# The first query block of an attention kernel: a split exponential, two projections placed earlier, a transpose on TensorE in place of DMA

## The chip, the core and the metric

The kernel runs on one core of a Trainium2 chip. The metric is the device time of one execution in microseconds (us); the time before is 1944.92 us, the median of three runs (1944.02 to 1945.15). Engines: PE (TensorE, matrix products into PSUM), ACT (ScalarE), DVE (VectorE), POOL (GpSimd) and SP (SyncE, here only an issuer of DMAs). They run their own instruction streams in order and wait for each other by semaphores.

## What is computed

x is 2048 rows of 640; there are 32 heads of width 192 with 2048 cached keys and values each.

```python
xn = layernorm(x)
q  = (xn @ wq), split into 32 heads of 192
p  = softmax(q @ k^T * 192**-0.5)
s  = (p @ v, heads joined) @ wo
h  = silu(xn @ w1) * (xn @ w3)
out = x + s * silu(h @ w2)
```

## The kernel before

**Tiles and stages.** The 2048 rows of x are four query blocks of 512, each of four row tiles of 128. Heads are worked one after the other; within a head the four query blocks; within a block eight *units* (p = 0 to 7), each of 256 keys. The list `stream` holds all 32 x 4 x 8 units, and n counts them; units 0 to 7 are head 0, block 0. After the heads come the rest of the gated FFN (L694 to L742) and the output product (L743 to L746).

**One unit.** `scores(n)` (L499, `emit_scores` L471) issues three pairs of products (L487, L488) into one PSUM tile of 1024 columns, then one exponential of the whole tile on ACT (L490), from PSUM into the bf16 tile pT2. Units 0 and 1 of the kernel begin with two full-height products (L483, L484) instead of two of the pairs. `values(n)` (L503) issues 16 products (L516) of pT2 with the values; the first eight read columns 0 to 511 of pT2 and the others columns 512 to 1023. The loop (L654) issues scores(n+2), then values(n), so the exponential runs while PE does other units. After unit 7 of a block DVE adds up the result (L525, L526) and scales it (L532, L533).

**PSUM turns.** The scores, every projection and the turned row tiles all take their PSUM tile from the pool `ps_st`, which has two buffers. A new tile there waits until the tile before the last has been read.

**x, normalized and turned.** For every row tile DVE computes statistics (`ln_stats`, L316, L317), POOL the reciprocal root (L327), DVE the normalized tile (`ln_norm`, L346). It then has to be transposed into `xnT`. In block 0 that is `ln_turn` (L349): ten PE products against an identity (L354) for two row tiles, then one copy from PSUM (L356). In the other blocks it is `ln_turn_dma` (L358): one transposing DMA for each row tile (L360), issued by SP. `swap_halves` (L362) then has SP copy both partition halves of a block crosswise into `xnS` (L364, L365).

**Projections.** `project0(qb)` (L403) makes the queries of head 0 for a block from xnT alone: ten full-height products (L410), a cast of one half on DVE (L429) and of the other on ACT (L430), and three DVE copies into `qC` (L413 to L415). `project(h, qb)` (L434) does it for a later head with 20 half-height products (L424) that read both xnT and xnS, the two casts, and three DMAs into qC that POOL issues (L377, L379). `project(1, 0)` is the one of head 1 for block 0; its result is first read by the scores of head 1.

**The order around the change.** It is written by hand (`tc.manual_schedule()`): each engine executes in the order in which the Python code issues.

- `head_start` (L571): loads, block 0 turned, project_first, scores(0), scores(1), statistics of block 1, its row tiles 0 and 1 normalized and their transposing DMAs issued. SP's queue in that order: the xnS copies of block 0, the second half of head 0's values, x of block 2, the two transposes, x of block 3.
- Unit 1 (`first_head`, L629): row tiles 2 and 3 of block 1 normalized, their two transposing DMAs, then swap_halves(1).
- Units 3 to 5: statistics of block 2 and the turning of its tiles 0 and 1; tiles 2 and 3 follow at unit 7.
- Unit 6: project0(1), then project(1, 0), then scores(8), the first scores of block 1, which read project0(1).
- Unit 8: project(1, 1), which reads xnT and xnS of block 1. Unit 12: project0(2).

**The check of the row sums.** After the last head DVE makes two columns of flags (L712 to L716); a product with a tile of ones (L717, L739) counts them, and the count decides at the end whether an exact second pass runs.

## Time and profile before

| what | value |
|---|---|
| time, median of 3 runs | 1944.92 us |
| the profiled execution's own time | 1944.92 us |
| its span in the profile | 1943.1 us |
| PE busy | 1928.0 us, 99% of the span |
| ACT, DVE, POOL busy | 1180.2, 653.6, 282.4 us |
| mean granted PE clock | 0.998 |

The span is what the hardware profiler saw from the first instruction to the last; 1.8 us of the time lie around it. "Busy" of an engine is the time in which it had at least one compute instruction in flight; matmuls overlap, so a busy PE is not a PE at its peak. In a timeline row the columns are start, duration, engine, line, operation, output<-inputs, shape and count; square brackets give the idle time of that engine just before the row and what ended it. In a row of DMA issues the last number is the time from issue to landing. The granted clock is the share of its full speed that TensorE was given.

### The profile page before, as it was taken

How to read it: one execution, taken by the hardware profiler on the slowest of the kernel's cores; microseconds unless marked ns; L12 is line 12 of the kernel's file. 1: busy time of each engine (PE TensorE's matmuls, PEld its weight loads, DVE VectorE, ACT ScalarE, POOL GpSimd, SP SyncE). 2: the span in 40 equal slices, each digit the busy share in tenths (PEclk: the TensorE clock that was granted, in tenths of full speed). 3: DMA queues.
4: the chain of work that ended last, by engine and by line, in shares of the span. 5: the costliest groups of instructions: out<-in, count | busy, mean ns of one | idle time of the engine just before them, and what ended most of it. 6: DMA issues, size and time to landing. Idle time of an engine off the chain costs nothing.

```text
span 1943.1 us, 59651 instructions
## 1 busy us (share of the span) xinstructions
PE 1928.0 (99%) x27263; PEld 1315.4 (68%) x27271; DVE 653.6 (34%) x996; ACT 1180.2 (61%) x1278; POOL 282.4 (15%) x501
## 2 busy tenths in 40 slices
PE   7999999999999999999999999999999999999998
PEld 5666666666666666666666666666666666577776
DVE  6433333333333333333333333333333334521111
ACT  5677676767676777676777777677767677210000
POOL 2111111111111111111111111111111110000000
PEclk9999999999999999999999999999999999999999
DMA  7743343323243434363434343434334220928882
GB/s 172 139 100 69 75 87 61 95 58 89 63 100 62 97 68 101 68 161 68 97 68 101 68 101 68 97 68 92 77 64 92 62 73 2 280 43 139 154 153 59
DMA packets 395987, 179.31 MB, mean 92 GB/s; under 512 B 342960, under 2 KB 384176, under 8 KB 395728
## 3 DMA queue, kind: packets, MB, share of 16 engines
q1 hardware_dynamic: 372480, 125.65, 31.2%
q0 software_dynamic: 19472, 45.71, 9.9%
q8 instruction: 215, 3.52, 0.8%
q10 hardware_dynamic: 3776, 4.06, 0.7%
q14 instruction: 44, 0.36, 0.1%
HBM read 52.82 MB, written 27.79 MB: 41 GB/s over the span
## 4 chain that ended last, share of the span: by engine, by line
PE 98%; DMA 1%; DVE 0%; ACT 0%; SPq 0%; issue 0%
PE obank L516 35%; PE st L487 33%; PE ps L424 14%; PE ps_s L111 11%; PE ps_f L728 3%; PE ps_gu L702 1%; DMA x_all<-in_A_x_dram 1%; PE st L488 1%; PE ps L410 0%; DMA xnT<-xn 0%; DVE stats L316 0%; ACT KW L277 0%; ACT xnT L356 0%; SPq L289 0%; PE pst L354 0%
## 5 line engine op out<-in xcount | busy, mean ns | idle before, releaser
L490 ACT ACTIVATE pT<-st 128x1024 bf16<-128x1024 f32 x1024 | 1046.2, 1022 | 249.8 <-PE st L488 234.2
L516 PEld LDWEIGHTS <-pT 64*128 64x128 bf16 x16384 | 711.4, 94 | 242.5 <-issue 0.4
L516 PE MATMUL obank<-vt,pT 64*128 64x193 bf16 x16384 | 849.5, 243 | 0.1
L487 PE MATMUL st<-qC,KW 64*128 64x512 bf16 x2046 | 605.6, 376 | 0.1
L525 DVE COPY osum<-obank 128x772 f32<-128x772 f32 x128 | 123.1, 962 | 789.0 <-PE obank L516 789.0
L488 PE MATMUL st<-qB,KW 64*128 64x512 bf16 x1024 | 385.0, 376 | 0.0
L487 PE MATMUL st<-qA,KW 64*128 64x512 bf16 x1022 | 384.3, 376 | 0.3 <-ACT pT L490 0.3
L488 PE MATMUL st<-qC,KW 64*128 64x512 bf16 x1022 | 384.3, 376 | 0.0
L488 PE MATMUL st<-qA,KW 64*128 64x512 bf16 x1022 | 384.3, 376 | 0.0
L487 PEld LDWEIGHTS <-KW 64*128 64x128 bf16 x3068 | 278.6, 94 | 153.2 <-issue 1.7
L424 PE MATMUL ps<-xnT,W 64*128 64x512 bf16 x1280 | 297.2, 376 | 0.0
L424 PE MATMUL ps<-xnS,W 64*128 64x512 bf16 x1280 | 296.4, 376 | 0.0
L488 PEld LDWEIGHTS <-KW 64*128 64x128 bf16 x3068 | 278.6, 94 | 0.6 <-issue 0.6
L377 POOL DMA_DIRECT2D qC<-qA x124 | 65.4, 527 | 1288.7 <-DVE rl_all L532 1269.0
L430 ACT CAST qB<-ps 128x512 bf16<-128x512 f32 x131 | 76.7, 585 | 235.0 <-PE ps L424 222.6
L111 PE MATMUL ps_s<-wo_sb,oT 128*128 128x384 bf16 (+3 forms) x1535 | 208.8, 299 | 0.1
L424 PEld LDWEIGHTS <-W 64*128 64x128 bf16 x2560 | 122.7, 94 | 122.2 <-issue 0.8
L111 PEld LDWEIGHTS <-oT 128*128 128x128 bf16 x1536 | 148.4, 98 | 60.4
L526 DVE TENSOR_TENSOR osum<-osum,obank 128x772 f32<-128x772 f32 x128 | 122.7, 959 | 13.4
L533 DVE TENSOR_TENSOR ostage<-osum,rl_all 128x768 bf16<-128x768 f32 x128 | 122.7, 958 | 4.5
L465 DVE SCALAR_TENSOR_TENSOR hT<-pt,qB 64x512 bf16<-64x512 bf16 x64 | 43.8, 684 | 198.3 <-ACT pt L464 198.3
L429 DVE CAST qA<-ps 128x512 bf16<-128x512 f32 x131 | 90.6, 692 | 30.2 <-PE ps L410 11.6
(84 smaller groups left out, 622.3 us busy)
## 6 DMA issues: line engine op xcount, KB each, us to landing
o_scr<-ostage SPq DMA_DIRECT2D x16, 1536.0 KB, 10.6
vt<-in_A_v_cache_dram SPq DMA_DIRECT2D x63, 384.0 KB, 6.0
qC<-qA POOLq DMA_DIRECT2D x248, 64.0 KB, 1.9
qC<-qB POOLq DMA_DIRECT2D x124, 64.0 KB, 2.4
wo_sb<-in_A_wo_dram POOLq DMA_DIRECT2D x1, 7680.0 KB, 30.7
W<-in_A_wq_dram POOLq DMA_DIRECT2D x32, 160.0 KB, 3.6
W<-in_B_w_dram POOLq DMA_DIRECT2D x32, 80.0 KB, 3.3
W<-in_A_wq_dram POOLq DMA_DIRECT2D x32, 80.0 KB, 3.0
```

The costliest lines, as they stand in the source:

```text
L111: nc.tensor.matmul(ps[:, 0:w], lhsT=oT[:, k, :], rhs=wo_sb[:, k, c0:c1], start=(k == 0), stop=(k == OC - 1))
L377: nc.gpsimd.dma_start(out=qC[0:64, half, :], in_=qAB[half][64:P, :])
L424: nc.tensor.matmul(ps[:, r * 512:(r + 1) * 512], lhsT=W[rows, j, :], rhs=xs[rows, j // 2, qs], start=(j == 0), stop=(j == 2 * DC - 1))
L429: a = nc.vector.tensor_copy(out=qAB[0][:], in_=ps[:, 0:512])
L430: b = nc.scalar.copy(out=qAB[1][:], in_=ps[:, 512:1024])
L487: nc.tensor.matmul(st2[:, 0:512], lhsT=ka, rhs=qa, start=r == 0 and nr == 3, stop=r == nr - 1)
L488: nc.tensor.matmul(st2[:, 512:1024], lhsT=kb, rhs=qb2, start=r == 0 and nr == 3, stop=r == nr - 1)
L490: nc.scalar.activation(out=pT2[:], in_=st2[:], func=ACT.Exp, scale=att_scale)
L516: nc.tensor.matmul(obanks[r][:, j * 256:j * 256 + DH + 1], lhsT=pT2[r * 64:(r + 1) * 64, t * 512 + j * P:t * 512 + (j + 1) * P], rhs=vt[r ...
L525: nc.vector.tensor_copy(out=osum[:], in_=ov[0])
L526: nc.vector.tensor_tensor(out=osum[:], in0=osum[:], in1=ov[1], op=ALU.add)
L533: nc.vector.tensor_tensor(out=ostage[:, qb * 4:qb * 4 + 4, hg * DH:(hg + 1) * DH], in0=osum[:, :, 0:DH], in1=rl.unsqueeze(2).to_broadcast( ...
```

## The change

Five edits:

1. The very first exponential (head 0, block 0, unit 0) is issued as two, of 512 columns each; all others stay whole.
2. In the first turn of the loop (n = 0) values(0) is issued ahead of scores(2); in all other turns scores come first, as before.
3. Row tiles 2 and 3 of block 1 are turned by PE and a DVE copy (`ln_turn(1, 1, ...)`), after values(3), in place of the two transposing DMAs after values(1). swap_halves(1) moves with it, from unit 1 to unit 3.
4. project(1, 0) moves from unit 6 to unit 3 (ahead of scores(5)), and project0(1) from unit 6 to unit 5 (ahead of scores(7)).
5. The tile of ones is 128 x 128 instead of 128 x 2, and the count is a product 128 x 2 instead of 2 x 2; row 0 is read as before.

```diff
         pT2 = pp.tile([P, 1024], BF16, tag="pT2", name="pT2")
-        nc.scalar.activation(out=pT2[:], in_=st2[:], func=ACT.Exp, scale=att_scale)
+        parts = 2 if (h, qb, p) == (0, 0, 0) else 1
+        w = 1024 // parts
+        for c in range(parts):
+            nc.scalar.activation(out=pT2[:, c * w:(c + 1) * w], in_=st2[:, c * w:(c + 1) * w], func=ACT.Exp, scale=att_scale)
...
         if qb == 0 and p == 1:
-            for i in (2, 3):
-                ln_norm(1, i, nc.vector)
-                ln_turn_dma(1, i)
-            swap_halves(1)
+            ln_norm(1, 2, nc.vector)
+            ln_norm(1, 3, nc.vector)
         if qb == 0 and p == 3:
             ln_stats(2, 0)
+            ln_turn(1, 1, nc.vector.tensor_copy)
+            swap_halves(1)
...
-        if h == 0 and qb + 1 < NQB and p == (6 if qb == 0 else 4):
+        if h == 0 and qb == 0 and p == 3:
+            project(1, 0)
+        if h == 0 and qb + 1 < NQB and p == (5 if qb == 0 else 4):
             project0(qb + 1)
-        if h == 0 and qb == 0 and p == 6:
-            project(1, 0)
-        scores(n + 2)
-        values(n)
+        for step in (values, scores) if n == 0 else (scores, values):
+            step(n + 2 if step is scores else n)
...
-    ones = fsb.tile([P, 2], BF16, tag="ones", name="ones")
+    ones = fsb.tile([P, P], BF16, tag="ones", name="ones")
...
-            nc.tensor.matmul(cnt[0:2, 0:2], lhsT=ones[:], rhs=okb[:], start=True, stop=True)
+            nc.tensor.matmul(cnt[:, 0:2], lhsT=ones[:], rhs=okb[:], start=True, stop=True)
```

On PE the order from unit 3 on becomes: project(1, 0), scores(5), values(3), the ten turning products, scores(6), values(4), project0(1), scores(7), values(5), scores(8), values(6), scores(9), values(7), project(1, 1). On DVE the cast of project(1, 0) and the copy of the turned tiles come ahead of most of block 2's statistics, with one row tile's statistics between them. On SP the two xnS copies of block 1 come straight after the load of x's block 3, ahead of all transposes of block 2. On POOL the three qC DMAs of project(1, 0) come ahead of block 2's reciprocal roots.

## The prediction

> **What bounds the kernel now.** First the page's busy line and chain of waits: PE is busy for 99% of the span and 98% of the chain. So time can only be won where PE is idle, slowed, or does less.

> ```profile
> PE 1928.0 (99%) x27263; PEld 1315.4 (68%) x27271; DVE 653.6 (34%) x996; ACT 1180.2 (61%) x1278; POOL 282.4 (15%) x501
> ...
> PE 98%; DMA 1%; DVE 0%; ACT 0%; SPq 0%; issue 0%
> ```

> Second, the table of waits: PE's only long one is a single wait at L410, in project0(1). Third, the timeline there, then PE's clock in short stretches (columns: stretch, length, busy us of the five engines, granted clock, DMA share, GB/s).

> ```profile
> 22.59 0.85 PE L516 MATMUL obank<-vt,pT 64*128 64x193 bf16 x16
> ...
> 28.69 0.58 PE L410 MATMUL ps<-xnT,W 128*128 128x512 bf16 x1 [5.25 <-DMA xnT<-xn]
> 29.50 3.59 PE L410 MATMUL ps<-xnT,W 128*128 128x512 bf16 x8 [0.22 <-issue]
> ...
> 45.46 2.33 PE L410 MATMUL ps<-xnT,W 128*128 128x512 bf16 x9
> ```
> ```profile
> 24.40:25.40 1.00, 0.00 (x0) 0.00 (x0) 0.93 (x4) 0.01 (x1) 0.05 (x1) 1.00 0.07 12
> 25.40:26.40 1.00, 0.00 (x0) 0.00 (x0) 0.97 (x4) 0.00 (x0) 0.64 (x1) 0.85 1.01 410
> 26.40:27.40 1.00, 0.00 (x0) 0.00 (x0) 1.00 (x3) 0.00 (x0) 0.00 (x0) 0.50 1.17 297
> ...
> 30.40:31.40 1.00, 1.00 (x4) 0.39 (x3) 0.00 (x0) 0.00 (x0) 0.00 (x0) 0.50 0.96 202
> ...
> 33.00:33.50 0.50, 0.50 (x7) 0.25 (x8) 0.37 (x1) 0.38 (x1) 0.00 (x0) 1.00 1.22 202
> ```

> PE stops at 23.44, 5.25 us long, for the last of block 1's transposing DMAs. And it pays twice: its clock halves at about 26.1 (a stretch with mean 0.85 is 0.7 at 1.0 and 0.3 at 0.5) and is back only near 32.9, so project0(1) takes 4.4 us (28.69 to 33.08) against 2.2 for the same product at 45.46. The hole is worth 5.25 + 2.2 = 7.45 us. Fourth, SP's transfers, by their issue and landing:

> ```profile
> 11.55 0.61 SPq L365 DMA_DIRECT2D xnS<-xnT  x1
> xnS<-xnT SPq DMA_DIRECT2D x1, 320.0 KB, 8.5
> ```
> ```profile
> 19.40 1.21 SPq L360 DMA_TRANSPOSE xnT<-xn  x1
> xnT<-xn SPq DMA_TRANSPOSE x1, 6.3
> ```

> Block 0's second xnS copy lands at 11.55 + 8.5 = 20.05. Block 1's transposes land at 23.5, 25.7 (19.40 + 6.3), 27.7 and 28.55. These landings are the limits of the new order.

> **Price list.** Scores of a unit 0.65 us (three pairs, 0.21 each in the chain, 0.216 with its gaps); values 0.67; project and project0 2.16; exponential 1.02; turning products 0.72 for ten (second L354 group), their copy 0.82 (L356 on DVE). A unit is 1.32 on PE, more than the exponential, so ACT follows PE.

> **Edits 1 and 2 (split exponential, values(0) first).** ACT starts at 14.07. Halves of 128x512 are not in the trace; the nearest rows are the casts of that size, 0.585, so the two end at 15.24 if nothing overlaps, against 15.09 whole. PE can begin values(0) when scores(1) is issued, 14.8, do eight products until 15.15, wait for the second half, and end at 15.6; scores(2) to 16.25; scores(3) waits for exponential 1, 16.25; from there 1.32 per unit. Unit 3 begins at 18.88 instead of 19.08: 0.2 won. Bounds: 0.15 us lost (ACT's extra work lands on the path whole) to 0.35 won (the 0.28 idle before scores(2) and the gaps after it). But what follows is a wait with a fixed end, so edits 1 and 2 are worth nothing in the sum; only were that wait gone would 0.2 show.

> **Edit 4, first half (project(1, 0) at unit 3).** In the profile it never waited, at 33. Now PE reaches it at 18.88 and its second product reads xnS of block 0, landed at 20.05; PE restarts about 0.1 later (28.55 to 28.69 in the chain), 20.15. A new wait of 1.27 us. Its weights landed at 17.0 (9.60 + 7.4). All that feeds this copy is issued before 12.2, ahead of every edit, so I keep its landing. Queued behind the waiting product: everything on PE, thus exponential 5.

> **Edit 3 and the rest, on PE from 20.15.** project(1, 0) to 22.31; scores(5) 22.96; values(3) 23.63; turning, new, 0.72, to 24.35 (its buffer is free when the casts of project(1, 0) end, 23.1); scores(6) 25.00 (exponential 5, after the cast on ACT, ends at 24.2); values(4) 25.67. It no longer meets the landing of the second half of the values at 21.2, which in the profile held values(4) for 0.36 us.

> Then project0(1), which needs two things. The DVE copy of the turned tiles: DVE casts 22.4 to 23.1, has one tile's statistics ahead (1.05; its x landed at 22.84), is free at 24.25, copies 24.5 to 25.35. And the second transposing DMA, landed at 25.7: PE starts at 25.80, a wait of 0.13, ends at 27.96. I take 25.7 although two transposes behind it are gone; bounds 25.0 (it moves no more once these are gone, and the DMA engines were nearly idle from 24.4 to 25.4) to 27.0 (the POOL copies of project(1, 0), 64 KB each and 1.9 to 3.0 from issue to landing, now share the DMA engines from 23.1 on; half of 2.7 if they hold it up).

> scores(7) and values(5) to 29.28. scores(8) needs the casts and the three qC copies. In the profile, project(1, 0) lay between and hid them; that cover of 2.16 is now 1.32. DVE reaches the cast only at 28.45 (statistics and two normalizations of block 2 are ahead), the third copy ends 1.54 later (33.13 to 34.67 in the profile), 29.99, so the last pair ends at 30.27 instead of 29.93: 0.34 lost; bounds 0.1 (DVE on time) to 1.1 (one more statistics group late). values(6), scores(9), values(7): 32.26.

> There project(1, 1) starts; in the profile at 37.82. **Won: 37.82 - 32.26 = 5.56 us.** In other words: the hole's 7.45, plus 0.36 and 0.2, less the new waits 1.27, 0.13 and 0.34 and the turning 0.72.

> **What is late next.** project(1, 1) reads xnS of block 1: SP issues its copies when both the second DMA and the DVE copy are in, 25.8 and 26.4; with the 3.6 and 4.5 us that they took in the profile they land by 30.9, 1.4 ahead. Behind them in SP's queue are block 2's transposes, 2 us earlier than before for the first two; the last two follow unit 7's DVE work (L525, L526, L346) at the same distance as before. They must land before project0(2). In the profile the last was issued at 41.73, took 3.5, landed at 45.2, and PE came at 45.46: 0.2 us spare, which I expect to hold, being five units of the same order later. POOL's qC copies of project(1, 0) are first read at head 1. From unit 8 on all engines' orders are unchanged.

> **Edit 5.** The count is one product: the ACT rows of L733 around it are 3.47 apart (1693.41 to 1696.88) instead of 3.26, so it costs 0.21 on PE. Its weight load goes from 2 to 128 columns: 0.08 to 0.098 by the rows; bounds 0.2 won to 0.1 lost; I take 0. The larger memset (0.06 for 2 columns, 0.20 for 128 x 128 on POOL) lies in DVE's 0.36 us of idle time before L734; without that cover 0.14.

> [...] PE's clock survived the idle 1.02 us before the first turning products (clock 1.00 from 5 to 10) and fell 2.7 us into the long hole. So waits of 1.27 and 0.13, five us apart, should leave it up. [...]

> **Rivals.**
> - *The clock falls all the same*, since waits of 1.27, 0.13 and 0.34 and the turning crowd into 11 us. Price: the 2.2 us that ten halved products lost; 1941.6. Against it: the clock held from 5 to 18 with PE busy 83 to 93%.
> - *The landings slip.* Every us that the xnS copy or the second transpose lands later costs 1 us: both are on the path, nothing covers them. At 1.7 us the change is within 0.2%; about 1941.5 to 1943.
> - *Slower: the hole moves to block 2.* Its transposes had 0.2 us to spare and now stand behind xnS copies that wait for a DVE copy. If the last lands 8.5 us after issue (as that xnS copy did) instead of 3.5, PE stands 4.8, the clock falls (2.2 more): +7.0 - 5.56 = +1.4, 1946.3. It decides from 3.6 us of lateness on (3.4 of standing and 2.2). Against: at 34 us of the new order the queue is as empty as at 40 of the old one.

> **How the numbers follow.** Against the profiled execution's own 1944.92 (span 1943.1 and 1.8 around it), also the median: 1944.92 - 5.56 = 1939.4. Its own range, by the bounds, 1938.4 to 1940.9. Chances: main case 0.83, clock 0.07, landings 0.07, block 2 0.03. The range reaches to the clock's case: 1938.3 to 1941.7. 0.2% is 3.9 us, about what a measurement tells from no change; below 1941.0 lie the main case and a little of the others: faster 0.85, same 0.12, slower 0.03.

> **What would show it.** No wait of PE over 1.5 us behind unit 0; one of about 1.3 us at L424 ended by the xnS copy, near 20.1; project0(1) of 2.2 us at clock 1.00, starting near 25.8; project(1, 1) near 32.3. Wrong if a clock of 0.5 appears, or if a wait over 2 us stands before project0(2).

## The result and the profile after

The changed kernel takes 1938.31 us, the median of six runs (1937.68 to 1938.64), against 1944.88 for the kernel before beside it (1943.27 to 1945.15): a ratio of 0.9968, 95% interval 0.9955 to 0.998. That is 6.6 us won; 1939.4 was forecast, with a range of 1938.3 to 1941.7. The profiled execution took 1938.20 us; its span is 1936.4, 6.7 less than before.

The busy line of the page after:

```profile
PE 1926.6 (99%) x27273; PEld 1315.6 (68%) x27281; DVE 654.6 (34%) x997; ACT 1180.0 (61%) x1279; POOL 282.5 (15%) x501
```

PE's busy time fell by only 1.4 us (1928.0 before), though the span fell by 6.7: the rest was idle time. The timeline after, with SP's second xnS copy of block 0, its second transposing DMA of block 1, the two projections, the turning and, last, project(1, 1); then the landings of that copy and of that DMA:

```profile
11.57 0.61 SPq L365 DMA_DIRECT2D xnS<-xnT  x1
...
18.84 0.38 PE L424 MATMUL ps<-xnT,W 64*128 64x512 bf16 x1
19.05 0.39 PE L424 MATMUL ps<-xnS,W 64*128 64x512 bf16 x2
...
19.42 1.20 SPq L360 DMA_TRANSPOSE xnT<-xn  x1
...
22.61 0.73 PE L354 MATMUL pst<-ident_bf,xn 128*128 128x128 bf16 x10
...
24.84 2.32 PE L410 MATMUL ps<-xnT,W 128*128 128x512 bf16 x9
...
31.04 0.38 PE L424 MATMUL ps<-xnT,W 64*128 64x512 bf16 x1
```
```profile
xnS<-xnT SPq DMA_DIRECT2D x1, 320.0 KB, 7.4
...
xnT<-xn SPq DMA_TRANSPOSE x1, 5.3
```

No row has the brackets of a long wait any more. project0(1) starts at 24.84 instead of 28.69 and takes 2.3 us instead of 4.4. PE's clock in the stretches that held the hole (columns as in the prediction):

```profile
24.00:26.00 2.00, 1.87 (x23) 1.13 (x21) 1.93 (x7) 1.02 (x1) 0.44 (x2) 1.00 0.95 360
26.00:28.00 2.00, 2.00 (x20) 0.87 (x19) 1.89 (x6) 0.58 (x1) 0.31 (x1) 1.00 1.08 213
```

The granted clock stays at 1.00. Two landings differ from the forecast. The xnS copy landed at 11.57 + 7.4 = 18.97, not at 20.05, so project(1, 0) went on at 19.05 after 0.2 us instead of 1.27. The second transposing DMA landed at 19.42 + 5.3 = 24.7, not at 25.7, so project0(1) could start at 24.84, though PE came to it 1.1 us earlier than forecast. project(1, 1) starts at 31.04, 6.78 earlier than in the profile before (37.82).

### The profile page after: what moved, and what is told of

It is laid out like the page before. It is cut to its first block, busy times and chain, and to the rows that moved or that the text cites. A ratio compares the mean times of both kernels' runs of the same rounds, so it can differ in the third digit from the quotient of the medians.

```text
span 1936.4 us, 59669 instructions
## 1 busy us (share of the span) xinstructions
PE 1926.6 (99%) x27273; PEld 1315.6 (68%) x27281; DVE 654.6 (34%) x997; ACT 1180.0 (61%) x1279; POOL 282.5 (15%) x501
## 4 chain that ended last, share of the span: by engine, by line
PE 99%; DVE 1%; DMA 0%; ACT 0%; issue 0%; DVEq 0%; ACTq 0%
PE obank L519 35%; PE st L487 34%; PE ps L424 14%; PE ps_s L111 11%; PE ps_f L731 3%; PE ps_gu L705 1%; PE st L488 1%; PE ps L410 0%; DVE stats L316 0%; DMA x_all<-in_A_x_dram 0%; PE ps L391 0%; PE pst L354 0%; PE pk L271 0%; DVE xn L346 0%; ACT pT L493 0%
## 5 line engine op out<-in xcount | busy, mean ns | idle before, releaser
L493 ACT ACTIVATE pT<-st 128x1024 bf16<-128x1024 f32 (+1 forms) x1025 | 1046.1, 1021 | 250.2 <-PE st L488 234.0
L424 PE MATMUL ps<-xnT,W 64*128 64x512 bf16 x1280 | 297.2, 376 | 0.0
L424 PE MATMUL ps<-xnS,W 64*128 64x512 bf16 x1280 | 296.0, 376 | 0.0
L424 PEld LDWEIGHTS <-W 64*128 64x128 bf16 x2560 | 122.9, 94 | 121.4 <-issue 0.2
```

What stands on the lines that cost most here:

```text
L424: nc.tensor.matmul(ps[:, r * 512:(r + 1) * 512], lhsT=W[rows, j, :], rhs=xs[rows, j // 2, qs], start=(j == 0), stop=(j == 2 * DC - 1))
L493: nc.scalar.activation(out=pT2[:, c * w:(c + 1) * w], in_=st2[:, c * w:(c + 1) * w], func=ACT.Exp, scale=att_scale)
```

## The experiments

**Edit 3 alone.** Which part carries the gain?

```diff
         if qb == 0 and p == 1:
-            for i in (2, 3):
-                ln_norm(1, i, nc.vector)
-                ln_turn_dma(1, i)
-            swap_halves(1)
+            ln_norm(1, 2, nc.vector)
+            ln_norm(1, 3, nc.vector)
         if qb == 0 and p == 3:
             ln_stats(2, 0)
+            ln_turn(1, 1, nc.vector.tensor_copy)
+            swap_halves(1)
```

> Edit 3 alone: row tiles 2 and 3 of block 1 turned by PE at unit 3, both projections still at unit 6, first exponential whole, count as before. Theory (the hole is one wait for two transposing DMAs plus the halved clock that follows it, and edit 3 removes both): PE reaches project0(1) near 24.2 and waits 0.5 to 1.6 us for the second of the two DMAs that remain, clock 1.00 throughout, project0(1) 2.2 us; 4.6 to 6.2 us faster than before, 1938.7 to 1940.3. Rival (the gain is the earlier place of project(1, 0), which fills the hole): at most 2.5 us faster.

1939.69 us against 1944.33, ratio 0.9977 (0.9968 to 0.9987): 4.6 us, at the lower edge of what the theory gave and far over the rival's 2.5. Its timeline:

```profile
21.03 0.81 PE L354 MATMUL pst<-ident_bf,xn 128*128 128x128 bf16 x10 [0.27 <-DVE xn L346]
...
23.96 0.37 PE L487 MATMUL st<-qA,KW 64*128 64x512 bf16 x1 [0.70 <-DVE xnT L356]
25.39 2.33 PE L410 MATMUL ps<-xnT,W 128*128 128x512 bf16 x9
```

Without project(1, 0) at unit 3, the turning comes before DVE has the row tile (0.27 idle), and the scores after it wait for DVE's copy out of the shared PSUM pool (0.70). The wait of 0.5 to 1.6 us that was expected at project0(1) itself did not come: the second transposing DMA landed at 23.4, before PE was there. project0(1) again takes 2.3, and the clock stays at 1.00. So taking two row tiles off the DMA path is most of the gain. The remaining 1.4 us to the changed kernel is the other edits together; that the move of project(1, 0) fills just these two waits is how the rows read, and was not measured by itself.

**The hole kept, PE kept running in it.** Is the slow product after the hole the clock's doing? The added products are extra work, overwritten at once.

```diff
         ps = ps_st.tile([P, 1024], F32, tag="st2", name="ps0")
+        for i in range(24 if qb == 1 else 0):
+            nc.tensor.matmul(ps[:, 0:512], lhsT=W[:, 0, :], rhs=xnT[:, 0, 0:512], start=True, stop=True)
```

> The kernel before, with 24 products of 512 columns (5.2 us) issued ahead of project0(1) into the same PSUM tile and then overwritten: extra work in the hole, nothing else. Theory (the 4.4 us of project0(1) after the hole are the halved clock, price 2.2 us): the wait for the last transposing DMA stays, the clock stays at 1.00, project0(1) takes 2.2; 1.2 to 2.2 us faster than before, 1942.7 to 1943.7, although PE does more. Rival (project0(1) is slow for another reason, such as reading xnT just written): no faster than before, or slower.

1942.65 us against 1944.33, ratio 0.9992 (0.9983 to 1.0001). The time alone just fails to exclude no change; the rows do not leave it open:

```profile
23.58 5.35 PE L409 MATMUL ps<-xnT,W 128*128 128x512 bf16 x23
28.77 2.32 PE L412 MATMUL ps<-xnT,W 128*128 128x512 bf16 x10
```
```profile
26.00:27.00 1.00, 1.00 (x6) 0.46 (x5) 1.00 (x3) 0.00 (x0) 0.00 (x0) 1.00 1.28 287
27.00:28.00 1.00, 1.00 (x6) 0.48 (x5) 0.93 (x4) 0.00 (x0) 0.00 (x0) 1.00 0.12 27
```

project0(1) (L412 here) starts as late as ever, at 28.77, and takes 2.32 instead of 4.4, at a clock of 1.00. Its price, about 2 us of the hole's 7.45, is shown. The time shows less of it (1.7), since in this trace the last transposing DMA landed at 27.84 and the added products held PE for some 0.8 us more. So xnT was not quite as freshly written here as before; but in the changed kernel's trace project0(1) starts 0.14 us after its DMA's landing, just as before (28.55 to 28.69), and takes 2.32 too. That rules the rival out.

**Edit 4 alone.** Does filling the hole from the front help, if the DMA path stays?

```diff
-        if h == 0 and qb + 1 < NQB and p == (6 if qb == 0 else 4):
+        if h == 0 and qb == 0 and p == 3:
+            project(1, 0)
+        if h == 0 and qb + 1 < NQB and p == (5 if qb == 0 else 4):
             project0(qb + 1)
-        if h == 0 and qb == 0 and p == 6:
-            project(1, 0)
```

> Edit 4 alone: project(1, 0) at unit 3 and project0(1) at unit 5, all four row tiles of block 1 still by transposing DMA. Theory (the end of the hole is the landing of the fourth transpose, 27.5 to 28.6, whatever lies before it, and a wait of over 2.7 us halves the clock): a wait of 3.2 to 4.7 us, project0(1) at half clock; 0.3 to 1.6 us faster than before. Rival (the clock stays up, since the hole is shorter): 2.6 to 3.7 us faster.

1944.8 us against 1944.33, ratio 1.0003 (0.9994 to 1.0012): nothing won, though 0.3 to 1.6 was expected.

```profile
29.26 0.59 PE L410 MATMUL ps<-xnT,W 128*128 128x512 bf16 x1 [4.79 <-DMA xnT<-xn]
30.06 3.62 PE L410 MATMUL ps<-xnT,W 128*128 128x512 bf16 x8 [0.22 <-issue]
```

The wait is 4.79, since the last transposing DMA landed only at 29.12 in this trace; with all four DMAs it landed between 27.69 and 28.68 in the others. The clock is at half from PE's return at 29.26 until 34.2, 5.0 us, longer than in any other trace here. The rival, a clock that stays up, is out. Edit 4 depends on edit 3: 4 without 3 is worth nothing, 3 without 4 and the others leaves 1.4 us.

**Edits 1 and 2 alone, and taken away.**

```diff
-        nc.scalar.activation(out=pT2[:], in_=st2[:], func=ACT.Exp, scale=att_scale)
+        parts = 2 if (h, qb, p) == (0, 0, 0) else 1
...
-        scores(n + 2)
-        values(n)
+        for step in (values, scores) if n == 0 else (scores, values):
+            step(n + 2 if step is scores else n)
```

> Edits 1 and 2 alone: first exponential in two halves, values(0) ahead of scores(2). Theory (PE gets to unit 3 about 0.2 us earlier, and the hole, whose end is a landing, takes all of it): no difference, within 0.3 us of before; the hole starts 0.2 us earlier and ends at the same landing. Rival (the two exponentials cost ACT 0.15 us on the path, or the gain carries through): a shift of the whole span by 0.15 to 0.4 us, one way or the other.

On the kernel before: 1943.82 us against 1944.33, ratio 0.9998 (0.9989 to 1.0007), no difference. The hole swallows it:

```profile
28.01 0.38 PE L410 MATMUL ps<-xnT,W 128*128 128x512 bf16 x1 [4.79 <-DMA xnT<-xn]
28.56 3.45 PE L410 MATMUL ps<-xnT,W 128*128 128x512 bf16 x8 [0.17 <-issue]
```

Taken back out of the changed kernel (the same diff reversed):

> The changed kernel with edits 1 and 2 undone: first exponential whole, scores(2) ahead of values(0). Theory (what edits 1 and 2 win in front is kept, since no wait with a fixed end is left behind them but the 0.1 us for the second transposing DMA): PE idle 0.28 us before scores(2) again, project(1, 0) starts 0.2 us later, the whole 0.1 to 0.3 us longer than the changed kernel, 1938.4 to 1938.6: not to be told apart by time, only by PE's rows between 14 and 26 us. Rival (the two edits carry a good part of the gain): 0.6 us or more longer.

1938.47 us; the changed kernel in the same series, 1938.27. The 0.28 us of idle time is back:

```profile
15.45 0.37 PE L487 MATMUL st<-qA,KW 64*128 64x512 bf16 x1 [0.28 <-ACT pT L490]
...
19.38 0.38 PE L424 MATMUL ps<-xnT,W 64*128 64x512 bf16 x1
...
25.09 2.32 PE L410 MATMUL ps<-xnT,W 128*128 128x512 bf16 x10
```

Counted from the first scores' product (13.39 here, 13.10 in the changed kernel), project(1, 0) starts after 5.99 instead of 5.74: 0.25 us. But project0(1) starts after 11.70 here and 11.74 in the changed kernel: there the two landings had taken the 0.25 back. So in these two traces edits 1 and 2 win nothing that lasts, against the theory that their gain is kept. In time the two kernels cannot be told apart, as expected.

**Edit 5 alone.**

```diff
-    ones = fsb.tile([P, 2], BF16, tag="ones", name="ones")
+    ones = fsb.tile([P, P], BF16, tag="ones", name="ones")
...
-            nc.tensor.matmul(cnt[0:2, 0:2], lhsT=ones[:], rhs=okb[:], start=True, stop=True)
+            nc.tensor.matmul(cnt[:, 0:2], lhsT=ones[:], rhs=okb[:], start=True, stop=True)
```

> Edit 5 alone on the kernel before: tile of ones 128 x 128, count product 128 x 2. Theory, as read from the changed kernel's trace (the ACT rows of the FFN around the count stand 3.28 us apart there, 3.47 before): the same 3.28 here, so 0.2 us less on PE; the time 0 to 0.4 us shorter, within the spread of the kernel before. Rival (the wider weight load costs its 0.02 us and nothing is won): 3.47 or 3.49.

1943.94 us against 1943.97, ratio 1.0 (0.9991 to 1.0009). In the trace of this run, the ACT rows ahead of, at and after the count:

```profile
1688.89 0.49 ACT L733 ACTIVATE ft<-ps_f 128x384 bf16<-128x384 f32 x1 [1.76 <-PE ps_f L728]
...
1691.78 0.10 PEld L739 LDWEIGHTS <-ones 128*128 128x128 bf16 x1
...
1692.15 0.49 ACT L733 ACTIVATE ft<-ps_f 128x384 bf16<-128x384 f32 x1 [1.76 <-PE cnt L739]
...
1695.43 0.49 ACT L733 ACTIVATE ft<-ps_f 128x384 bf16<-128x384 f32 x1 [1.79 <-PE ps_f L728]
```

They are 3.26 and 3.28 apart; before, 3.26 and 3.47. So 0.19 us is won although 64 times as many weight columns are loaded (0.10 instead of 0.08 us). What went is a pause ahead of the load; the row in the trace before was

```profile
1693.24 0.08 PEld L739 LDWEIGHTS <-ones 128*2 128x2 bf16 x1 [0.26 <-issue]
```

Why the narrow load had this pause of 0.26 us and the wide one none was not tried.

**The changed kernel once more.**

> The changed kernel once more, unchanged, for its spread and for a second look at the landings. Theory (the xnS copy's 20.05 in the one profiled execution of the kernel before was about 1 us later than usual, and the wait of 1.27 us that the prediction built on it does not come): xnS lands near 19.0, no wait over 0.3 us at project(1, 0), time 1937.7 to 1938.8. Rival (the landing differs from execution to execution by 1 us or more): a wait of up to 1.3 us at project(1, 0) in this profile, and a spread of the times of more than 1.5 us.

1938.27 us, median of seven (1938.07 to 1939.32), against 1943.97: ratio 0.997 (0.9959 to 0.9981). The profiled one of the seven is the slowest, 1939.32, and it is the one that settles the matter:

```profile
11.82 0.61 SPq L365 DMA_DIRECT2D xnS<-xnT  x1
...
19.10 0.38 PE L424 MATMUL ps<-xnT,W 64*128 64x512 bf16 x1
20.47 0.39 PE L424 MATMUL ps<-xnS,W 64*128 64x512 bf16 x2 [0.99 <-DMA xnS<-xnT]
...
26.11 2.33 PE L410 MATMUL ps<-xnT,W 128*128 128x512 bf16 x10
...
32.33 0.38 PE L424 MATMUL ps<-xnT,W 64*128 64x512 bf16 x1
```
```profile
xnS<-xnT SPq DMA_DIRECT2D x1, 320.0 KB, 8.6
```

Here the copy lands at 20.42, PE stands between 19.10 and 20.47 as forecast (0.99 of it not covered by the product in flight), and project(1, 1) starts at 32.33; the forecast said 32.26, and 1939.4 for the whole. So the rival of this run holds in its main point: the landing differs from execution to execution (the times spread by 1.25 us, less than the 1.5 that it named). The traces of all kernels that issue this copy in this place give two groups: 20.05 and 20.42 (the kernel before, this run), and 18.9 to 19.5 in the eight others. PE came to project0(1) after the second transposing DMA here (24.47), without a long wait.

**A later xnS copy.** Is it true that nothing covers project(1, 0) in its new place? The first attempt exchanged the wrong pair:

```diff
+        load_v(0, (1,))
         swap_halves(0)
...
-        load_v(0, (1,))
         load_x(2)
```

> The changed kernel with one pair of SP's issues exchanged: the second half of head 0's values (384 KB) ahead of the two xnS copies of block 0. Theory (in its new place project(1, 0) has no cover: every us that the xnS copy lands later than about 19 is one us on the path): the copies land 1.3 to 2.1 us later, near 20.3 to 21.1; PE waits 1.3 to 2.1 us at project(1, 0), of which the 0.1 us wait before project0(1) gives back its part; 1.1 to 2.1 us longer than the changed kernel, 1939.4 to 1940.4; the clock stays at 1.00. Rival (the queue is shared anyway, the landing does not move, or the wait before project0(1) takes its place): within 0.4 us of the changed kernel.

1941.47 us (1939.42 to 1944.43), ratio 0.9989 (0.998 to 0.9998). It does not answer the question: SP no longer holds this load behind the wait for block 0's turning, so it is issued before 10 us (at 12.22 in the changed kernel's trace), and the first scores begin 1.5 us later, at 14.82. That the load competes with the first ones is a reading that no run shows by itself. The second attempt puts the load between the two copies, where it can start no earlier:

```diff
         nc.sync.dma_start(out=xnS[0:64, :, qs], in_=xnT[64:P, :, qs])
+        if g == 0:
+            load_v(0, (1,))
         nc.sync.dma_start(out=xnS[64:P, :, qs], in_=xnT[0:64, :, qs])
```

> The changed kernel with the second half of head 0's values (384 KB) issued between the two xnS copies of block 0 instead of behind both; no load starts earlier than in the changed kernel. Theory (project(1, 0) in its new place has no cover: what the second xnS copy lands late is on the path one for one): that copy is issued 1.2 us later and lands 1 to 2 us later than in the changed kernel's own executions (19.0 or 20.4); PE waits 1.3 to 3 us at L424; 1.0 to 2.6 us longer than the changed kernel, 1939.3 to 1940.9; clock 1.00. Rival (the wait only takes the place of others behind it): within 0.4 us of the changed kernel.

1942.65 us (1939.98 to 1945.09) against 1944.3, ratio 0.9992 (0.9983 to 1.0001), 4.4 over the changed kernel: more than expected.

```profile
12.41 1.79 SPq L367 DMA_DIRECT2D xnS<-xnT  x1
...
22.96 0.39 PE L426 MATMUL ps<-xnS,W 64*128 64x512 bf16 x2 [3.56 <-DMA xnS<-xnT]
```
```profile
23.00:24.00 1.00, 1.00 (x8) 0.48 (x9) 0.00 (x0) 0.00 (x0) 0.00 (x0) 0.80 0.17 36
...
25.00:26.00 1.00, 1.00 (x8) 0.44 (x6) 0.00 (x0) 0.00 (x0) 0.00 (x0) 0.50 0.98 355
```

The copy took 10.5 us from its issue and landed at 22.9, some 2.5 to 4 us late instead of 1 to 2. PE stood for all of it, 3.56 us, and then the clock fell too, at 23.6, when PE had been back at work for 0.6 us. The mechanism holds (no cover, one for one), the sizes do not: here the wait brought the clock's price with it. In this trace project(1, 1) starts at 36.51, 5.5 us later than in the changed kernel's; the longer wait is 3.7 of it and the 3.4 us of work at half clock (0.50 granted) cost 1.7, half of their length. The control is the same exchange on the kernel before:

> The same exchange on the kernel before. Theory: project(1, 0) stands behind the hole there, 12 us later, so the late copy costs nothing: within 0.5 us of the kernel before. Rival (the exchange itself costs, by the loads behind it): 1 us or more longer than the kernel before, and then the cost in the changed kernel is not that of the wait.

1945.75 us (1944.05 to 1946.87) against 1944.3, ratio 1.0006 (0.9997 to 1.0015): no difference that the interval can tell. But the medians differ by 1.4 us, and the interval reaches 2.9, so some of the 4.4 may be the exchange's own. Its hole is the old one:

```profile
28.81 0.59 PE L412 MATMUL ps<-xnT,W 128*128 128x512 bf16 x1 [5.48 <-DMA xnT<-xn]
```

So by the medians about 3 of the 4.4 us belong to the lost cover and the clock; the rows above, 3.7 and 1.7 in one execution, are the better evidence.

**What is left behind the change.** In the changed kernel's trace DVE reaches the cast of project(1, 1) 0.7 us late (34.06, PE's end 33.37), which holds scores(11) for 0.3 us.

```diff
-                if p == ((4, 7) if qb == 0 else (3, 5))[i2]:
+                if p == ((4, 6) if qb == 0 else (3, 5))[i2]:
...
+        if n == 5:
+            first_head(qb, p)
         if p == (5 if h == 0 else 2) and h < 2 * NPIG:
             swiglu(h, qb)
...
-        if h == 0:
+        if h == 0 and n != 5:
             first_head(qb, p)
```

> The changed kernel with block 2's last statistics ahead of swiglu(0, 0) on DVE at unit 5, and row tiles 2 and 3 of block 2 normalized at unit 6 instead of 7. Theory (in the changed kernel the cast of project(1, 1) waits on DVE behind the block's sums and these two normalizations, and holds scores(11) for 0.3 us): that wait goes; 0.2 to 0.4 us shorter than the changed kernel, 1937.9 to 1938.1, to be seen in PE's rows and hardly in the time. Rival (DVE's earlier work comes between the sums and PE): no gain, or 0.1 to 0.5 us longer.

1938.4 us (1937.87 to 1940.13) against 1944.3, ratio 0.9971 (0.996 to 0.9983): not to be told apart from the changed kernel. From project0(1) to project0(2) it is 13.93 us (24.93 to 38.86) instead of 14.02 in the changed kernel's trace: 0.1 us, not the 0.2 to 0.4 expected, and the time does not show it. No version here beats the changed kernel by more than its spread.

## Why the prediction was right

**The number: at the edge.** 1938.31 lies just inside the lower end of the range (1938.3) and below the 1938.4 that the prediction's own bounds give; the median of the repeat, 1938.27, lies just outside. What the runs confirm is the mechanism.

**The hole and its two prices: right.** Wait and half clock were both taken away, by edit 3 (alone: no wait at project0(1), 2.33 us at a clock of 1.00); the run that kept PE running in the hole shows the clock's part by itself (2.32 us instead of 4.4).

**"All that feeds this copy is issued before 12.2, ahead of every edit, so I keep its landing": the step that was off.** The term was 1.27 us of waiting at project(1, 0); in the trace after it is 0.2. That the edits do not move the landing fits the traces: each of the two groups above holds traces with edits 3 and 4 and without them. That one execution gives *the* landing was wrong: 20.05 belonged to the rarer, late group.

**The second transposing DMA at 25.7, at the earliest 25.0: also off.** It landed at 24.70 in the trace after and 24.47 in the late one, and at 24.8 to 25.1 in four traces that keep all four DMAs, so 25.7 too was a late draw. The short wait before project0(1), about 0.2 us against the 0.13 forecast, came out right by luck: PE and this DMA were both about 1 us earlier. Had the DMA landed at 25.7, PE would have waited there for most of what the early xnS copy had won.

**Like with like.** In the one late trace of the kernel before, the hole ended late as well: its last DMA landed at 28.55, against 27.69 to 27.87 in three early traces with the same order of DMAs (PE kept running in the hole, edits 1 and 2 alone, edit 5 alone). Late execution against late execution: 1944.92 - 1939.32 = 5.60 us, against 5.56 forecast. That is one execution of each, and small terms cancel in it: the first scores began 0.27 us later in the changed kernel's (13.36 against 13.09), which the terms below, scores(8) and edit 5, make up for. The medians are further apart, 6.57 in the first series and 5.70 in the one with the repeat, so 5.56 was a little low.

**scores(8) waiting for the qC copies, 0.34: too large.** From project0(1) to project(1, 1) is 6.20 us in the trace after and 6.22 in the late one, against 6.12 by the price list: 0.1. DVE reached the cast 0.05 us after PE's end (28.49 in the late one), not 0.49 (28.45 against 27.96): from the start of its copy of the turned tiles to the cast it took 3.7 us there, 3.95 in the sum.

**Edit 5, 0: 0.19 won**, at the far bound that the prediction kept.

**The other terms held.** Unit 3 was reached at 18.84 (18.88 forecast), the turning took 0.73 (0.72). Edits 1 and 2 win 0.25 up to project(1, 0) (0.2 forecast) and, in these traces, nothing that lasts, neither on the kernel before nor in the changed one. The clock rival did not come: the clock was 1.00 in every stretch from 14 to 40 of the trace after and from 14 to 30 of the late one, with the turning in both and a wait of 0.99 in the late one. That waits this short and the turning together bring the clock down, which sets the upper end of the range, is shown by no run. project(1, 1)'s own xnS copy had less room than the 1.4 us forecast: 25.52 + 5.3 = 30.8, and PE came at 31.04. In block 2, project0(2) starts at 38.86, 0.24 after its last DMA, as expected, so the slower rival did not come either. After unit 8 the changed kernel loses 0.3 us against the sum, part of it at scores(11). Added up, 5.56 + 1.07 (first copy) + 0.24 (scores(8)) + 0.19 - 0.3 is 6.8, against 6.7 between the spans of the two profiles.

**Two readings to put right.** The idle 1.02 us that the clock survived and the 0.36 us that held values(4) are rows of the weight loads. PE's own row stands 0.85 us ahead of the first turning products, and values(4) began about 0.2 us late. The sum by starting times uses neither.

## What to carry to other kernels

When a step waits for a transfer near the start, one profile gives one draw of the landing: price the step by several executions, or carry a spread of a us for it (here landings from 18.9 to 20.42 in ten traces), and compare late with late. An idle stretch of TensorE can cost more than its length (in the kernel before 5.25 us, and about 2 more in the slowed product): in these traces the clock fell with each of the six waits of 3.56 us and more, and with none of those up to 1.80. Taking work off the transfer's path onto an engine that would stand idle anyway (here ten small products, 0.7 us) bought back both, 4.6 us by edit 3 alone. An edit can be worth nothing alone and something behind another: here moving work into the hole could pay only once the end of the hole was no longer a late landing.

## What was not expected of the hardware

**The clock was down for 3.4 us in three traces and for 6.8 us in three.** From the clock in short stretches of the traces: in the kernel before it was at half from 26.1 to 32.9, with the late copy on the kernel before from 26.0 to 32.9, in edit 4 alone from 27.4 to 34.2, all 6.8 us; in edits 1 and 2 alone from 28.3 to 31.7, in edit 5 alone from 28.15 to 31.55, with the late copy in the changed kernel from 23.6 to 27.0, all 3.4. For edits 1 and 2 alone the ends of the stretch are in these rows (a mean of 0.80 is 0.3 us at full clock and 0.2 at half):

```profile
28.00:28.50 0.50, 0.38 (x1) 0.20 (x3) 0.30 (x2) 0.00 (x0) 0.08 (x1) 0.80 0.00 0
...
31.50:32.00 0.50, 0.50 (x4) 0.06 (x4) 0.00 (x0) 0.00 (x0) 0.00 (x0) 0.79 1.01 225
```

**Landings came in two groups.** The same copy, behind the same issues, landed near 19.0 (18.9 to 19.5 in eight traces) or about 1.2 us later (20.05 and 20.42 in two); the copy ahead of it (18.54 and 19.00 in the two late traces, 17.2 to 17.9 in the eight others) and the x load behind it (9.5 us in both late traces, 7.4 to 8.8 in the others) moved along. What decides between the two was not found.
